# Batch 1 of an attention kernel: q and k cast into SBUF and transposed on TensorE instead of by DMA, additive masks built on GpSimd

## The chip, the cores and the metric

One core of a Trainium2 chip runs the whole kernel. The time is the device time of one execution in microseconds. Before the change the median of 13 runs is 360.24 us (356.14 to 362.5). PE is TensorE's matmul side, PEld its weight loads, DVE is VectorE, ACT ScalarE, POOL GpSimd, SP SyncE (here it only issues DMAs).

## The reference

Attention over q, k, v of shape (8 batches, 8 heads, 576 positions, 64), then a feed-forward layer:

```python
scores = q @ k.T / 8                      # per batch and head
rel = pos[:, None] - pos[None, :]
plain:   0 <= rel < 32                    # heads 0 to 3
dilated: 0 <= rel < 128 and rel % 4 == 0  # heads 4 to 7
attn = softmax(where(mask, scores, -1e9)) @ v
x = attn, heads side by side              # 4608 tokens x 512
h = x @ w_in                              # 512 x 2048
out = (h * sigmoid(beta * h)) @ w_out     # 2048 x 512
```

Inputs and output are fp32; the kernel multiplies in bf16.

## The kernel before

**Stages.** A batch has 576 tokens; the feed-forward part runs over 9 groups of 512 tokens. For each group there are 16 h slots (`slot_h`: four matmuls of 512 columns, a tanh on ACT, line 486, and a multiply on DVE, line 489, that leaves `g`) and 16 o slots (`slot_o`: four matmuls each, line 512, scaled out by ACT, stored by SP). The attention of batch t + 1 is issued between the slots of group t, and batch 0 before them all. Every engine has its own queue and takes its instructions in the order in which the program issues them, so the order of work is the order in the code: lists of step names (`FIRST` for batch 0, `SECOND` for batch 1, `THIRD` for batch 2, `STEPS` for the rest) say in which order a batch's steps come, and the loop at the end says after which slot how many of them are issued (at t = 0 the function `first`, later a share by `WORK`). At t = 0 the slots are 16 h and 12 o; the first 21 have no step behind them, the next has 28, and each one after that 5.

**Steps.** A step is a letter and digits. x is a pair of heads: 0 and 1 plain, 2 and 3 dilated.
- `K`, `Q` (batch 0 only): q or k, already in SBUF as bf16 with tokens on the partitions (`tok`, loaded and cast by POOL's DMA queue, line 258), is transposed on PE (lines 344, 353) and copied out of PSUM into `kd`, `qzd` (dilated) or `k1`, `q1` (plain). K has one copy, on DVE or ACT. Q has two, one on DVE and one on ACT, into two halves whose rest is zero.
- `S`: a score tile, with exp on ACT (line 411). In batches 0 and 1 an additive mask (`neg`) is first put into PSUM by a matmul with the identity (line 386); from batch 2 on POOL multiplies the exp by a 0/1 mask instead (line 413).
- `V`: scores times v, with a column of ones for the sum; DVE takes the reciprocal (line 434) and multiplies (line 438).
- `X`: transposed on PE (line 448) and copied by ACT into `xT`, the input of the feed-forward part.
- `d`, `k`, `q` (batch 1 on): the spreads, DVE copies (lines 285, 289, 297) of DMA-transposed q and k into the zero-padded `qzd`, `kz`, `qq`. For these batches POOL's queue casts q and k into a scratch in HBM (`cast_qk`, line 245) and SP's queue transposes them from there into SBUF (lines 267, 276).
- `v`: v cast from its fp32 staging (`vd_st`, `vp_st`).
- `m0`, `m1`, `M0`: masks finished on DVE. POOL builds 0/1 masks (lines 165 to 200) and DVE turns them into additive ones (`negate`, line 162). `M0` also zeroes `kz[0]`, whose storage `k1` of batch 0 used.

The plain heads of batch 0 keep their keys and queries in natural order; from batch 1 on they are split into even and odd positions, as the DMA transpose gives them, which is why `mask_p` has an even and an odd part and a score tile of plain heads takes four matmuls (line 398) instead of two (line 392).

**Queues.** POOL issues the loads that cast; a load waits until the eighth before it has landed. `gate` is a one-element POOL copy that waits for a DMA transpose to land, so that the DMAs behind it in POOL's program don't start sooner.

Of the kernel before, what the change touches and what calls it, by code (L numbers as in the profile page):

```python
# [23 lines left out]
    "K2 K3 Q2 Q3 m0 S20 S21 S22 S23 v0 v1 K0 K1 m1 V20 S30 V21 S31 V22 S32 V23 S33 Q0 Q1 V30 S00 V31 "  # L24
    "X20 S01 V32 S02 V33 v2 S10 X21 S11 V00 X30 S12 V01 X31 V10 X00 V11 X01 X10 X11"
).split()
SECOND = (
    "M0 d0 d1 S20 S21 S22 S23 S30 S31 S32 S33 v3 k0 k1 V20 V21 V22 V23 q0 q1 q2 q3 V30 S00 V31 S01 "
    "X20 v2 V32 S02 V33 S10 X21 S11 V00 X30 S12 V01 X31 V10 X00 V11 X01 X10 X11"
# [8 lines left out]
def kernel(  # L38
# [10 lines left out]
    nc = tc.nc  # L49
# [41 lines left out]
    def bank(dt=FP32):  # L91
# [27 lines left out]
    k1 = kz[0][:].rearrange("p a b c d -> p (a b c d)")[:, 0:2 * (WIN + S)].rearrange(  # L119
        "p (x t) -> p x t", x=2)  # L120
    q1 = qq[0][:].rearrange("p a b c d -> p (a b c d)").rearrange("p (x h t) -> p x h t", x=2, h=2)
    plain_T = {n: const([P, c0 + 2 * S], BF16, f"{n}pT") for n, c0 in (("k", WIN // 2), ("q", 0))}
    xT = const([P, NKT, B * S], BF16, "xT")

# [3 lines left out]
    for m, (n, x) in enumerate((n, x) for n in "kq" for x in range(2)):  # L128
# [3 lines left out]
    mask_1, neg_1_pp, neg_1_fp = (  # L132
        xT[:, m, 2 * S:2 * S + 4 * QT].rearrange("p (a n) -> p a n", a=2) for m in range(3))
    neg_1 = {"FP": neg_1_fp, "PP": neg_1_pp}
# [8 lines left out]
    def zeros(i):  # L143
        if i == 0:
            for x in range(4):
                nc.vector.memset(pt[x][:, pt_w[x]:], 0.0)
            for x in range(2, 4):
                nc.vector.memset(pt[x][64:96, 8 * DQ[0]:8 * DQ[0] + 32], 0.0)
            nc.vector.memset(k1[:, :, 0:WIN], 0.0)
            nc.vector.memset(q1[64:128, :, 0], 0.0)  # L150
            nc.vector.memset(q1[0:64, :, 1], 0.0)
        nc.vector.memset(qzd[i][64:128, 0], 0.0)
        nc.vector.memset(qzd[i][0:64, 1], 0.0)
        if i:
            zeros_kz(i)
            nc.vector.memset(plain_T["k"][:, 0:WIN // 2], 0.0)
        nc.vector.memset(vp[i][:, :, :, D:D + 1], 1.0)
        nc.vector.memset(vd[i][:, :, :, :, D:D + 1], 1.0)


    def negate(t, m):
        nc.vector.tensor_scalar(
            out=t, in0=m, scalar1=-1.0, scalar2=NEG, op0=ALU.add, op1=ALU.mult)

    def build_masks_d():

        for hf, lo in ((0, 0), (1, DQ[0] - DO[1])):
            flat = mask_d[hf][:].rearrange("p a b n -> p (a b) n")
            nc.gpsimd.memset(flat, 1.0)
            nc.gpsimd.affine_select(  # L170
                out=flat, in_=flat, pattern=[[0, 4], [1, DQ[hf]]], base=lo,
                channel_multiplier=-1, compare_op=ALU.is_ge, fill=0.0)
            nc.gpsimd.affine_select(
                out=flat, in_=flat, pattern=[[0, 4], [-1, DQ[hf]]], base=WIN - 1 - lo,
                channel_multiplier=1, compare_op=ALU.is_ge, fill=0.0)


    def build_mask_1():
        flat = mask_1.rearrange("p a (b n) -> p (a b) n", b=2)
        nc.gpsimd.memset(flat, 1.0)  # L180
        nc.gpsimd.affine_select(
            out=flat, in_=flat, pattern=[[0, 4], [-1, QT]],
            base=-1, channel_multiplier=1, compare_op=ALU.is_ge, fill=0.0)
        nc.gpsimd.affine_select(
            out=flat, in_=flat, pattern=[[0, 4], [1, QT]],
            base=WIN, channel_multiplier=-1, compare_op=ALU.is_ge, fill=0.0)
# [14 lines left out]

    def finish_masks_1(b, n, eng):
        if n == 0:
            for hf in range(2):
                negate(neg[f"d{hf}"][:], mask_d[hf][:].rearrange("p a b n -> p a (b n)"))
        else:
            for n in ("PP", "FP"):
                negate(neg_1[n], mask_1)
            nc.vector.memset(neg_1["FP"][0:WIN, 0], -NEG)

    def finish_masks(b, n, eng):
        zeros_kz(0)
        pp, fp = mask_p["PP"], mask_p["FP"]
        nc.vector.tensor_copy(
            out=pp[64:128].rearrange("p a b e u -> p (a b) e u"), in_=mask_t[64:128])
        nc.vector.tensor_copy(out=fp[:], in_=pp[:])
        for e in range(2):
            nc.vector.memset(fp[64 * e:64 * e + WIN // 2, 0], 0.0)
        for n in ("PP", "FP"):
            negate(neg[n][:], mask_p[n][:].rearrange("p a b e u -> p a (b e u)"))  # L220
# [31 lines left out]
    def load_tok(n, x):  # L252
        dst = tok[n, x]
        R, T = (72, 8) if x else (64, 9)
        src = {"q": q, "k": k}[n][0, 4 * x:4 * x + 4].rearrange("h (a T) d -> a h (T d)", T=T)
        for lo, hi in ((0, 64), (64, R)):
            if lo < hi:
                nc.gpsimd.dma_start(out=dst[lo:hi], in_=src[lo:hi])
# [44 lines left out]
    def load_vp_1(eng, n, m, p=0):  # L303
        eng.dma_start(
            out=vp_st[0][:].rearrange("p h i d -> p (h i) d")[p:P, n:n + m],
            in_=bass.AP(tensor=v.tensor, offset=v[0, 0].offset + (QT * n - WIN + p) * D,
                        ap=[[D, P - p], [QT * D, m], [1, D]]))

# [26 lines left out]
    kd[0] = kd_pool.tile([P, 2, 4, CT], BF16, name="kdT")  # L335
# [22 lines left out]
    def step_k(b, x):  # L358
        eng = nc.scalar if x % 2 else nc.vector
        if x < 2:  # L360
            copy_on(eng)(out=k1[:, x, WIN:].rearrange("p (a e) -> p a e", e=9),
                         in_=transposes_p("k", x))
        else:
            copy_on(eng)(out=kd[0][:, x - 2].rearrange("p h (a w) -> p h a w", w=2),
                         in_=transposes_d("k", x - 2))

    def step_q(b, x):
        tv = transposes_p("q", x) if x < 2 else transposes_d("q", x - 2)
        for hf in range(2):
            rows = slice(64 * hf, 64 * hf + 64)  # L370
            out = (q1[rows, x, hf].rearrange("p (a e) -> p a e", e=9) if x < 2 else
                   qzd[0][rows, hf, x - 2].rearrange("p h (a w) -> p h a w", w=2))
            copy_on(nc.scalar if hf else nc.vector)(out=out, in_=tv[rows])

    def step_s(b, x, j):
# [8 lines left out]
        if b < 2:  # L384
            rhs = neg_1[key] if b == 0 and x < 2 else neg[key]
            nc.tensor.matmul(sc[0:K, :, 0:2 * n], lhsT=ident_b[0:K, 0:K], rhs=rhs[0:K],  # L386
                             start=True, stop=False)
        for a in range(2):
            if x < 2:
                i = 2 * j + a  # L390
                if b == 0:
                    nc.tensor.matmul(
                        sc[:, a, 0:2 * n], lhsT=k1[:, x, i * QT:i * QT + P],
                        rhs=q1[:, x, :, i * QT:(i + 1) * QT], start=False, stop=a == 1)
                    continue
                for h2 in range(2):
# [5 lines left out]
                        start=b > 1, stop=b > 1 or a + h2 == 2)  # L402
# [39 lines left out]
    def step_x(b, x, j):  # L442
# [10 lines left out]
        if x < 2 and b == 0:  # L453
# [11 lines left out]
    BRING = {"d": spread_dil, "k": spread_k, "q": spread_q, "v": cast_v, "m": finish_masks_1, "M": finish_masks}  # L465

    def attention_step(b, name):
        if name[0] in STEP:
            STEP[name[0]](b, *[int(c) for c in name[1:]])
        else:  # L470
            eng = (nc.scalar if b == 0 and name == "q0" or b == 1 and name == "v2" else
# [64 lines left out]
    def extras(b):  # L536
# [4 lines left out]
        if b + 1 < B:  # L541
# [7 lines left out]
            if b == 1:  # L549
                at("V21", load_vd, b + 1, G)  # L550
            name = "V21" if b > 2 else "S32" if b > 1 else "V30"
            for kind in "kq":
                at(name, load_dil, b + 1, kind)
            for kind in "kq":
                at(name, load_plain, b + 1, kind)
# [18 lines left out]
    V.memset(vp_st[0][0:WIN, 0, 0], 0.0)  # L574
    for n in "kq":
        load_tok(n, 1)
    make_identity(nc, ident_b[:])
    make_identity(nc, ident_f[:])
    load_vd(0, SQ)
    load_vp_1(SQ, 0, 1, WIN)  # L580
    load_vp_1(A, 1, 2 * NI - 1)
    SQ.dma_start(out=beta_row[:], in_=moe_beta.rearrange("(f p) -> f p", p=P))
    zeros(0)
    zeros(1)
    load_tok("k", 0)
    build_masks_d()
    load_tok("q", 0)
    load_vp_1(G, 2 * NI, 2 * NI)
    build_mask_1()
    for g in range(4):  # L590
        load_w_in(g)
    for name in FIRST:
        if name == "S33":
            build_beta()
        if name == "v2":
            G.memset(vd_st[64:96, 1], 0.0)
            build_masks_p()
        attention_step(0, name)
    for g in range(2):
        load_w_out(g)  # L600
    load_vd(1, G)
    for n in range(4):
        load_vp(1, G, n * NI, NI)
    for kind in "kq":
        cast_qk(1, kind)
    for kind in "kq":
        load_dil(1, kind)
    for kind in "kq":
        load_plain(1, kind)
    gate(raw[1, "d"][0:1, 0, 0, 0:1])  # L610
# [4 lines left out]
    for kind in "kq":  # L615
        cast_qk(2, kind)


    at_once = [3, 2] + [1] * (NTT - 3) + [4]
    WORK = {"S": 3, "V": 3, "X": 2, "d": 3, "k": 0, "q": 0, "v": 0, "M": 0}  # L620
    left = []
    first = lambda n: 0 if n < 21 else 28 + 5 * (n - 21)
# [62 lines left out]
```

## Time and profile before

| | us |
|---|---|
| median of 13 runs | 360.24 (356.14 to 362.5) |
| the profiled execution | 361.1 |
| its span in the trace | 359.3 |
| first matmul starts | 10.01 |
| first matmul of the feed-forward part | 32.0 |
| first matmul of group 1 | 72.7 |
| PE / DVE / ACT / POOL busy | 321.0 / 210.6 / 191.9 / 134.5 |

The page cuts the span into 40 slices of 9 us, with the busy share of each engine in tenths; the row PEclk is the granted clock of PE. The chain of work that ended last follows each piece of work back to what released it. A group of instructions is given with its line, engine, operation and tile, the number of instructions and their time; "[3.05 <-DVE qq L297]" says that the engine sat idle for 3.05 us before it, until line 297 on DVE had written `qq`. Starts are microseconds from the start of the span. Times of matmuls overlap, so that the distance from one start to the next says more of their rate than the length of one.

### The profile page before, as it was taken

Reading aid. Unit: us, or ns where it says so; the run is one execution under the profiler, and the core shown is the slowest. Engines: PE = TensorE matmul, PEld = TensorE weight load, DVE = VectorE, ACT = ScalarE, POOL = GpSimd, SP = SyncE. Lnnn points to the kernel's source line nnn. Section 1 sums busy time; section 2 is a strip of 40 time slices with the busy share of each in tenths; the row PEclk is TensorE's granted clock in tenths of the full one; section 3 lists DMA queues with packets and bytes.
Section 4 is the critical chain, followed back from the end, with each engine's and each line's share of the span. In section 5 each row is a group of like instructions: output and inputs, shape, how many; then the busy total and the mean of one; then the engine's idle time right before and its main releaser. Section 6 shows DMA issues by size and latency. Waiting matters only on the chain.

```text
span 359.3 us, 6041 instructions
## 1 busy us (share of the span) xinstructions
PE 321.0 (89%) x2265; PEld 169.0 (47%) x2265; DVE 210.6 (59%) x439; ACT 191.9 (53%) x365; POOL 134.5 (37%) x170
## 2 busy tenths in 40 slices
PE   0798996988867998799999999999999999999995
PEld 0674444534442554355545554555455544444442
DVE  6554787459894579356955693679356444334400
ACT  1455734666531676266656665666566555435511
POOL 8993045016273535353464355346333200000000
PEclk9998997899996999899999999999999999999999
DMA  8999999998976890799269928991101111111031
GB/s 173 208 206 212 169 151 204 196 216 168 192 121 132 168 194 0 161 163 176 52 128 182 193 50 161 189 197 31 35 29 31 30 30 31 58 30 31 29 80 66
DMA packets 67757, 43.77 MB, mean 122 GB/s; under 512 B 52288, under 2 KB 61712, under 8 KB 67280
## 3 DMA queue, kind: packets, MB, share of 16 engines
q1 hardware_dynamic: 58864, 25.99, 37.0%
q0 software_dynamic: 7440, 17.04, 26.0%
q10 hardware_dynamic: 1424, 0.36, 0.6%
q8 instruction: 17, 0.28, 0.4%
q14 instruction: 12, 0.10, 0.1%
HBM read 39.32 MB, written 17.69 MB: 159 GB/s over the span
## 4 chain that ended last, share of the span: by engine, by line
PE 76%; DVE 15%; ACT 3%; DMA 2%; issue 1%; POOL 0%; DVEq 0%; ACTq 0%; POOLq 0%
PE h_ps L481 30%; PE o_ps L512 28%; DVE qq L297 4%; DVE xs L438 3%; PE at L431 3%; PE at L481 3%; PE h_ps L512 3%; PE at L448 3%; DVE g L489 3%; DMA xT<-in_k_dram 2%; PE at L405 2%; DVE kz L289 2%; PE at L398 2%; PE at L386 1%; ACT osb L517 1%
## 5 line engine op out<-in xcount | busy, mean ns | idle before, releaser
L489 DVE SCALAR_TENSOR_TENSOR g<-tnh,h_ps 128x512 bf16<-128x512 bf16 x132 | 90.2, 685 | 98.7 <-ACT tnh L486 98.2
L481 PE MATMUL h_ps<-xT,w_in_bf 128*128 128x512 bf16 x528 | 134.3, 383 | 3.5 <-DVE g L489 3.2
L512 PE MATMUL o_ps<-w_out_bf,g 128*128 128x512 bf16 x512 | 132.2, 387 | 3.3 <-ACT osb L517 3.2
L486 ACT ACTIVATE tnh<-h_ps,beta_half 128x512 bf16<-128x512 f32 x132 | 90.7, 687 | 61.9 <-PE h_ps L481 55.4
L512 PEld LDWEIGHTS <-g 128*128 128x128 bf16 x576 | 53.4, 99 | 58.5 <-issue 9.5
L481 PEld LDWEIGHTS <-w_in_bf 128*128 128x128 bf16 x576 | 53.3, 99 | 57.3 <-issue 7.8
L411 ACT ACTIVATE pt<-at 128x384 bf16<-128x384 f32 (+2 forms) x112 | 48.1, 440 | 29.1 <-PE at L398 13.5
L413 POOL TENSOR_TENSOR pt<-pt,mask_d 96x384 bf16<-96x384 bf16 (+1 forms) x48 | 35.7, 755 | 58.1 <-ACT pt L411 57.5
L438 DVE TENSOR_TENSOR xs<-at,rcp 96x256 bf16<-96x256 f32 (+2 forms) x96 | 44.5, 463 | 15.6 <-PE at L448 11.6
L413 POOL TENSOR_TENSOR pt<-pt,mask_PP 128x384 bf16<-128x384 bf16 x24 | 23.6, 982 | 36.4 <-ACT pt L411 36.3
L517 ACT ACTIVATE osb<-o_ps 128x512 f32<-128x512 f32 x32 | 19.1, 597 | 27.5 <-PE o_ps L512 27.5
L431 PEld LDWEIGHTS <-pt 128*128 128x128 bf16 (+2 forms) x448 | 25.8, 102 | 16.0 <-POOL pt L413 2.7
L448 PE MATMUL at<-ident_b,xs 96*128 96x96 bf16 (+1 forms) x224 | 20.0, 208 | 7.5 <-DVE xs L438 5.1
L297 DVE COPY qq<-qpT 64x1152 bf16<-64x1152 bf16 x28 | 24.8, 884 | 0.6
L448 PEld LDWEIGHTS <-xs 96*128 96x128 bf16 (+1 forms) x224 | 13.5, 100 | 18.4 <-DVE xs L438 10.5
L405 PEld LDWEIGHTS <-kdT 128*96 128x96 bf16 (+1 forms) x128 | 15.6, 130 | 12.0 <-issue 2.5
L431 PE MATMUL at<-vd,pt 96*128 96x65 bf16 (+1 forms) x256 | 19.9, 202 | 0.7 <-POOL pt L413 0.6
L458 ACT COPY xT<-at 128x288 bf16<-128x288 bf16 x28 | 10.8, 398 | 16.9 <-PE at L448 16.8
L405 PE MATMUL at<-qzd,kdT 128*96 128x192 bf16 (+1 forms) x128 | 19.1, 239 | 0.7 <-DVE qzd L285 0.7
L413 POOL TENSOR_TENSOR pt<-pt,mask_FP 128x384 bf16<-128x384 bf16 x12 | 12.8, 1063 | 15.6 <-ACT pt L411 15.6
L434 DVE RECIPROCAL rcp<-at 96x4 f32<-96x4 f32 (+2 forms) x96 | 16.6, 173 | 3.0 <-PE at L431 2.4
L398 PE MATMUL at<-qq,kz 128*128 128x96 bf16 x168 | 14.7, 213 | 3.0 <-DVE qq L297 3.0
(94 smaller groups left out, 221.6 us busy)
## 6 DMA issues: line engine op xcount, KB each, us to landing
qk<-in_k_dram POOLq DMA_DIRECT2D x7, 576.0 KB, 5.6
qk<-in_q_dram POOLq DMA_DIRECT2D x7, 576.0 KB, 8.0
vp_st<-in_v_dram SPq DMA_DIRECT2D x10, 384.0 KB, 8.6
vd_st<-in_v_dram SPq DMA_DIRECT2D x6, 384.0 KB, 5.1
w_in_bf<-in_moe_w_in_dram POOLq DMA_DIRECT2D x4, 512.0 KB, 9.5
w_out_bf<-in_moe_w_out_dram POOLq DMA_DIRECT2D x4, 512.0 KB, 7.8
out_dram<-osb SPq DMA_DIRECT2D x8, 256.0 KB, 3.0
vd_st<-in_v_dram SPq DMA_DIRECT2D x6, 320.0 KB, 6.3
```

The source lines that it names most:

```text
L297: copy_on(eng)(out=qq[b % 2][64 * hf:64 * hf + 64, :, :, e], in_=raw[b, "q"][64 * e:64 * e + 64].rearrange("p (h i u) -> p h i u", h=4, i=NI))
L405: nc.tensor.matmul(sc[0:K, a, 0:2 * n], lhsT=kd[b][:, rp, h4, DO[hf]:DO[hf] + K], rhs=qzd[b % 2][:, :, rp, h4, hf * DQ[0]:hf * DQ[0] + n], ...
L411: nc.scalar.activation(out=w, in_=sc[0:K, :, 0:2 * n], func=ACT.Exp, scale=SCALE)
L413: nc.gpsimd.tensor_tensor(out=w, in0=w, in1=mask[0:K], op=ALU.mult)
L431: nc.tensor.matmul(pv[:, a, h2, :], lhsT=pt[x][0:K, c:c + P], rhs=rhs, start=True, stop=True)
L438: nc.vector.tensor_tensor(out=xs_t[b, x, jx][:, a0:a0 + m], in0=pv[0:n, :, :, 0:D], in1=rcp[0:n, 0:m].unsqueeze(3).to_broadcast([n, m, 2, ...
L448: nc.tensor.transpose(xp[:, a * n:(a + 1) * n], xs[:, a].rearrange("p h d -> p (h d)"), ident_b[0:n, 0:n])
L481: nc.tensor.matmul(hps, lhsT=w_in_bf[:, kt, fb * P:(fb + 1) * P], rhs=xT[:, kt, t * NTOK:(t + 1) * NTOK], start=(kt == 0), stop=(kt == NKT ...
L486: nc.scalar.activation(out=tnh[:], in_=hps, func=ACT.Tanh, scale=beta_half[:, fb:fb + 1])
L489: nc.vector.scalar_tensor_tensor(out=g[:], in0=tnh[:], scalar=1.0, in1=hps, op0=ALU.add, op1=ALU.mult)
L512: nc.tensor.matmul(ops[:], lhsT=g_t[t, fb][:, tb * P:(tb + 1) * P], rhs=w_out_bf[:, fb, :], start=(fb == 0), stop=(fb == NFB - 1))
L517: nc.scalar.mul(out=osb[:], in_=ops[:], mul=0.5)
```

## The change

Batch 1 takes the path of batch 0. Its q and k are cast by POOL's queue straight into the `tok` tiles (which batch 0 has done with), and `SECOND` has K and Q steps in place of d, k, q and M. `k1` and `q1` become lists, one for each of the two buffers, so the plain heads of batch 1 too have natural order, two matmuls to a score tile and the copy of `xT` without the even and odd split. The additive masks are built whole by POOL, ahead of the first steps; the 0/1 masks, needed from batch 2 on, are built by POOL much later, and finished there instead of on DVE. `zeros(1)` moves on DVE's queue from the start to behind batch 0's attention; `kz[0]` is zeroed at step X11 of batch 1 and `kz[1]` at step S30 of batch 2. The load of v for batch 0's plain heads is one load on POOL's queue after the token tiles, where ACT's queue had one half and POOL's the other; plain v of batch 1 is one load instead of eight. In the POOL queue order the eight loads of `vp_st` for batch 2 and its two casts to HBM keep their place at the end; `v0`, `v1` come first in `FIRST`. At t = 0 the steps of batch 1 are issued four after each slot, from slot 15 on.

```diff
-    "K2 K3 Q2 Q3 m0 S20 S21 S22 S23 v0 v1 K0 K1 m1 V20 S30 V21 S31 V22 S32 V23 S33 Q0 Q1 V30 S00 V31 "
-    "X20 S01 V32 S02 V33 v2 S10 X21 S11 V00 X30 S12 V01 X31 V10 X00 V11 X01 X10 X11"
+    "v0 v1 K2 K3 Q2 Q3 S20 S21 S22 S23 S30 S31 K0 K1 S32 V20 S33 V21 Q0 Q1 V22 V23 S00 V30 "
+    "S01 V31 X20 S02 v2 V32 S10 V33 X21 S11 V00 X30 S12 V01 X31 V10 X00 V11 X01 X10 X11"
 ).split()
 SECOND = (
-    "M0 d0 d1 S20 S21 S22 S23 S30 S31 S32 S33 v3 k0 k1 V20 V21 V22 V23 q0 q1 q2 q3 V30 S00 V31 S01 "
-    "X20 v2 V32 S02 V33 S10 X21 S11 V00 X30 S12 V01 X31 V10 X00 V11 X01 X10 X11"
+    "K2 K3 Q2 Q3 v0 v1 S20 S21 S22 S23 K0 K1 S30 V20 S31 V21 S32 V22 S33 V23 Q0 Q1 V30 S00 "
+    "V31 X20 v2 S01 V32 S02 V33 S10 X21 S11 V00 X30 S12 V01 X31 V10 X00 V11 X01 X10 X11"
...
+    def band(t, w, lo, hi, yes, no):
+        flat = t.rearrange("p a (b n) -> p (a b) n", n=w)
+        nc.gpsimd.memset(flat, yes)
+        nc.gpsimd.affine_select(
+            out=flat, in_=flat, pattern=[[0, 4], [1, w]], base=-lo,
+            channel_multiplier=-1, compare_op=ALU.is_ge, fill=no)
+        nc.gpsimd.affine_select(
+            out=flat, in_=flat, pattern=[[0, 4], [-1, w]], base=hi,
+            channel_multiplier=1, compare_op=ALU.is_ge, fill=no)
...
+    def build_neg_d():
+        for hf, lo in enumerate(LO):
+            band(neg[f"d{hf}"][:], DQ[hf], -lo, WIN - 1 - lo, 0.0, -NEG)
...
+    def build_neg_p():
+        band(neg["PP"][:], QT, -WIN, -1, 0.0, -NEG)
+        nc.gpsimd.tensor_copy(out=neg["FP"][:], in_=neg["PP"][:])
+        nc.gpsimd.memset(neg["FP"][0:WIN, 0], -NEG)
...
-                if b == 0:
+                if b < 2:
                     nc.tensor.matmul(
-                        sc[:, a, 0:2 * n], lhsT=k1[:, x, i * QT:i * QT + P],
-                        rhs=q1[:, x, :, i * QT:(i + 1) * QT], start=False, stop=a == 1)
+                        sc[:, a, 0:2 * n], lhsT=k1[b][:, x, i * QT:i * QT + P],
+                        rhs=q1[b][:, x, :, i * QT:(i + 1) * QT], start=False, stop=a == 1)
...
             if b == 1:
-                at("V21", load_vd, b + 1, G)
+                at("X20", load_vd, b + 1, G)
+                at("X11", zeros_kz, 0)
+            if b == 2:
+                at("S30", zeros_kz, 1)
...
+    load_vd(0, SQ)
+    load_vp_1(0, SQ, 0, 1, WIN)
+    SQ.dma_start(out=beta_row[:], in_=moe_beta.rearrange("(f p) -> f p", p=P))
     for n in "kq":
-        load_tok(n, 1)
+        load_tok(0, n, 1)
     make_identity(nc, ident_b[:])
...
-    zeros(0)
-    zeros(1)
-    load_tok("k", 0)
-    build_masks_d()
-    load_tok("q", 0)
-    load_vp_1(G, 2 * NI, 2 * NI)
-    build_mask_1()
+    for n in "kq":
+        load_tok(0, n, 0)
+    build_neg_d()
+    load_vp_1(0, G, 1, 4 * NI - 1)
+    build_neg_p()
     for g in range(4):
         load_w_in(g)
+    make_identity(nc, ident_f[:])
+    zeros(0)
     for name in FIRST:
         if name == "S33":
             build_beta()
...
     for g in range(2):
         load_w_out(g)
+    for x in (1, 0):
+        for n in "kq":
+            load_tok(1, n, x)
+    G.memset(vd_st[64:96, 1], 0.0)
     load_vd(1, G)
-    for n in range(4):
-        load_vp(1, G, n * NI, NI)
-    for kind in "kq":
-        cast_qk(1, kind)
-    for kind in "kq":
-        load_dil(1, kind)
-    for kind in "kq":
-        load_plain(1, kind)
-    gate(raw[1, "d"][0:1, 0, 0, 0:1])
+    load_vp_1(1, G)
+    zeros(1)
+    V.memset(plain_T["k"][:, 0:WIN // 2], 0.0)
     for g in range(2, 4):
         load_w_out(g)
     for n in range(4):
         load_vp(2, G, n * NI, NI)
     for kind in "kq":
         cast_qk(2, kind)
+    build_masks_d()
+    build_masks_p()
...
-    first = lambda n: 0 if n < 21 else 28 + 5 * (n - 21)
+    first = lambda n: 0 if n < 15 else 4 * (n - 14)
```

## The prediction

> **What bounds the kernel now.** I read the top of the page first, then the work of each engine in cut-out stretches, then the chain that ended last, then the engines' own rows in order of time.
>
> ```profile
> span 359.3 us, 6041 instructions
> PE 321.0 (89%) x2265; PEld 169.0 (47%) x2265; DVE 210.6 (59%) x439; ACT 191.9 (53%) x365; POOL 134.5 (37%) x170
> PE   0798996988867998799999999999999999999995
> PEclk9998997899996999899999999999999999999999
> ```
>
> From slice 13 on (about 115 us) PE is at 9 in every slice: the steady state, bound by matmuls, 34.3 us per group of 512 tokens. The change touches nothing there. Whatever it does, it does in the first 115 us, which I cut at PE's own boundaries: A, until the first transpose at 10.0; B, attention of batch 0 (10.0 to 32.7); C, sixteen h slots of group 0 (to 47.56); D, twelve o slots of group 0 with attention of batch 1 among them (47.56 to 72.83); E, group 1 with attention of batch 2 (72.83 to 115.4). The stretches (columns: length, then busy time and count of PE, PEld, DVE, ACT, POOL, then clock, DMA share, GB/s):
>
> ```profile
> 47.56:72.83 25.27, 21.22 (x187) 12.70 (x186) 16.32 (x43) 11.15 (x26) 10.28 (x15) 0.86 1.06 193
> 72.83:115.40 42.57, 33.28 (x238) 16.98 (x236) 33.10 (x58) 20.75 (x41) 19.31 (x21) 0.94 0.87 162
> ```
>
> In D, PE has much less to do than its 21.22 us say. At full rate 4 matmuls of 512 columns take 0.86 us (chain), so 12 o slots are 10.4. Attention by its warm cadences: dilated scores with their masks 2.0 (53.36 to 55.37), plain ones 6 x 0.33, V 8 x 0.12 and 4 x 0.18, X about 1.2: 6.9. That is 17.3 of 25.3; 8.0 us are lost. The chain says to what (start, length, what):
>
> ```profile
> 48.30 0.69 DVE g L489
> ...
> 49.20 0.70 DVE kz L140
> ...
> 53.29 1.42 DVE vd L330
> ...
> 59.59 0.47 DVE qq L297
> 60.05 0.04 issue
> 60.09 0.48 PE at L398 x4
> ```
>
> For 11.8 us (48.30 to 60.05) DVE alone carries the end: zeroing kz, finishing masks, spreading the DMA-transposed q and k. PE then runs dry, and afterwards runs at half rate. The PE rows show both (start, busy, then shape; in brackets the wait):
>
> ```profile
> 13.79 0.53 PE L405 MATMUL at<-qzd,kdT 128*96 128x192 bf16 x2
> 53.52 0.33 PE L405 MATMUL at<-qzd,kdT 128*96 128x192 bf16 x2
> 60.09 0.48 PE L398 MATMUL at<-qq,kz 128*128 128x96 bf16 x4 [3.05 <-DVE qq L297]
> 61.55 1.91 PE L512 MATMUL h_ps<-w_out_bf,g 128*128 128x512 bf16 x4
> ```
>
> The same pair takes 0.53 in B and 0.33 in D (0.32 against 0.165 start to start). B is at half rate from 10 to 27.9 although the clock row gives it 9; and the o slot at 61.55 takes 1.71 on the chain for 0.86. So D's 8.0 is 3.05 of wait, about 3.2 of half rate (60.1 to 66.5), and 1.7 of small waits.
>
> **The change, part by part.** *A: the first loads.* The load of 352 KB on ACT's queue goes; its data joins a POOL load behind the four token tiles. Rows 5 to 10 us moved 212 GB/s, so 352 KB in front of k's landing (the chain's 7.72 us of DMA) are worth up to 1.7. Bounds 0 and 1.7; I take 1.4, since it did start ahead of k (0.98 against 1.33) and landed at 8.2, before k at 9.9. v0 and v1 now stand ahead of K2 in DVE's queue and wait for vd_st: its halves landed 4.0 and 6.7 us after their issues, at 4.8 and 8.0 or so, and earlier without the 352 KB; two casts of 0.68 are over before K2 has anything to copy (k's landing plus 0.7). Hidden, with about 1 us to spare; later by more than that it would delay K2 one for one. The POOL issues moved up (q's plain tile past the masks, 0.6) are behind k's in the queue.
>
> *B: masks.* The additive masks come from POOL in the 2.5 us that the multiplicative ones took (5.40 to 8.05), so DVE's four negations and a memset (0.36, 0.42, 0.22 in groups) vanish. PE's wait of 1.19 on neg_d is replaced by a wait for ACT's half of qzd, which ended at 13.3 with scores starting at 13.99: 0.6 gained. Six scores now run before K0, and V22, V23 between Q1 and S00, where PE waited 0.41 and 0.26: 0.3 more. Matmul counts don't change. I take 0.9 (0.5 to 1.5). POOL's v2 cast waits for the bigger vp load: the bytes ahead of it are the same 2.6 MB, so about 16 us as now, needed by V00 at 25.
>
> *C.* zeros(1), some 3.1 us by its rows 4.71 to 8, moves behind batch 0's last DVE work, where DVE waited 3.16 for the first tanh. Nothing; without that cover the first g would be late by up to 3 us, of which the two-deep banks and 0.17 of slack per g would return 2.7 by C's end.
>
> *D.* Out: M0 (two memsets, three copies and so on), the spreads d, k, q of 0.94, 1.35 and 1.85, on DVE; four DMA transposes on SP (41.4 to 50), whose data landed up to 53, and POOL's gate of 12.0 us. In: six token loads (1152 KB) behind w_out. By 205 GB/s after vp (16 us) come w_in 2048, w_out 1024, these 1152: landed near 36.5, vd_st at 40, vp_st at 44. They are needed at 46 and after, so also the waits for eight loads outstanding on POOL's queue are covered. In on PE: 104 transposes. 32 of 72 columns: between 0.035 (half of B's 0.070) and 0.070; 72 of 64 columns: between 0.030 (the warm V matmuls: six in 0.18) and 0.042 (B). 3.3 to 5.3 us, I take 3.7, warm. In on DVE: two copies of 0.70 and four of 0.70, 4.3; on ACT two of 0.64 and four of 0.65, 3.9. PE needs 17.3 + 3.7 = 21.0. What it still waits for: S20 needs K2, Q2, Q3 through DVE, then ACT's half after DVE's half (as at 12.66). From the last h slot, t0: tanh and g 1.4, K2 2.1, Q2 2.8, ACT's half 3.5. PE has transposes 1.3, one o slot 0.86 and a mask 0.16 for it, until 2.35: waits 1.15, and 0.4 for S21. Later an o slot stands between every four steps, and DVE (14.2 us with V's divisions) and ACT (13.6) keep up; some 0.9 for the tail of X. D is 23.5 instead of 25.3: 1.8 gained.
>
> [...] The row: 17.9 us of nearly unbroken small matmuls at half rate (10 to 27.9), and again 6.5 us after the gap at 57. [...]
>
> *E.* Zeroing kz: one pair (2 x 0.70) at D's end, where DVE waited 3.71: nothing. The other pair stands at S30 of batch 2, in a stretch where DVE is the bound (33.1 of 42.6 busy, 9.6 of 10 from 80 to 90). It delays every g and V behind it, and PE waits for g. DVE has 1.2 us idle from 94 to 97 to give back. 0.2 to 1.4, or 3.1 if it tips a half-rate window; I take 1.0. Batch 2's casts end near 58 instead of 69, and its transposes follow earlier, but nothing in E waited for them (DVE's qzd at 80.24 had no wait ahead): 0. The multiplicative masks, 5 to 6 us of POOL after those casts, are over by 60; first used at 82. SP's queue holds nothing else then.
>
> **Sum.** -1.4 - 0.9 - 1.8 + 1.0 = -3.1. The profiled execution took 361.1 (span 359.3, 1.8 around it): 358.0. It lies 0.9 above the median of 360.24, so the forecast for a median is 357.1. The runs of before spread from 356.1 to 362.5, in two clumps; 0.5% (1.8 us) is about what can be told from no change.
>
> **Rivals.** *D at half rate (slower).* Its place is D's first 14 us, small matmuls between o slots. [...] For it: B's row. Against: after o slots came back at 65.4 the rate was full. *The gain stays on paper (same).* k lands at 9.9 anyway because its own small pieces, not the 352 KB, set it, and D stays at 25.3 as the copies' hand-over DVE to ACT eats the shorter DVE chain: -0.9 + 1.0 = about 0, 360.3; with A real, 358.9. For it: k took 8.3 us for 256 KB, more than its bytes need. [...]
>
> **How the numbers follow.** The main case 0.46, paper 0.22, half rate 0.19, more 0.13. Faster by over 0.5%: nearly all of the main case and of the last, 0.59; same 0.22; slower 0.19. The main case alone spans 355.3 to 358.9. The range takes in the fast rival's time and the paper rival, and stops between it and the half-rate rival: 353.5 to 362.0.
>
> **What would show it.** First transpose at 8.6 rather than 10.0 (A). First h slot near 30.4 (B). From the last h slot to the first h of group 1, 23.5 us, 512-column matmuls at 0.216 each, no PE wait over 1.5 and none on a spread (D). E 43.6, with DVE still the releaser. The prediction is wrong if token tiles of batch 1 land after 46, if o slots in D take 1.7, or if E grows by more than 2.

## The result, and the profile after

The median fell from 360.14 us (48 runs, 356.14 to 362.5) to 353.43 us (11 runs, 350.65 to 356.19). The ratio is 0.9815, with a 95% interval of 0.9774 to 0.9855: faster by 1.9%, some 6.7 us, where 3.1 was forecast. The sign is right, but less than half of the gain was forecast: 353.43 lies just under the range's low end of 353.5.

The top of the page of the kernel after (busy time of each engine, then PE's busy tenths and the granted clock in 40 slices):

```profile
span 351.7 us, 6237 instructions
PE 316.8 (90%) x2357; PEld 168.6 (48%) x2357; DVE 208.9 (59%) x430; ACT 195.8 (56%) x371; POOL 135.9 (39%) x178
PE   0998989986768997999999999999999999999995
PEclk9999999999998999999999999999999999999999
```

PE executes 92 more matmuls and yet is busy 4.2 us less: its matmuls have become shorter, not fewer. The clock row says why. Before, five of its digits were under 9 (slices 3, 6, 7, 12 and 16, counted from 0); now one is.

I cut both profiled executions at the same places of PE's program:

| stage | before | after | change | forecast |
|---|---|---|---|---|
| A, to the first transpose | 10.01 | 8.47 | -1.54 | -1.4 |
| B, attention of batch 0, to the first h | 21.99 | 20.01 | -1.98 | -0.9 |
| C, sixteen h slots | 15.38 | 14.25 | -1.13 | 0 |
| D, twelve o slots with batch 1 | 25.29 | 24.03 | -1.26 | -1.8 |
| E, group 1 with batch 2 | 42.70 | 43.52 | +0.82 | +1.0 |
| group 2 | 35.79 | 33.39 | -2.40 | 0 |
| groups 3 to 8 | 208.14 | 208.03 | -0.11 | 0 |
| span | 359.3 | 351.7 | -7.6 | -3.1 |

Two of the three surprises, C and group 2, are in stretches where PE runs the same matmuls in the same order in both kernels. In group 2 the rows differ in nothing but the rate. Here are the last two o slots of groups 1 and 2, eight equal matmuls each, of the kernel before (PE's rows in order of time: start, busy, shape, count):

```profile
111.96 3.62 PE L512 MATMUL o_ps<-w_out_bf,g 128*128 128x512 bf16 x8
147.86 3.44 PE L512 MATMUL o_ps<-w_out_bf,g 128*128 128x512 bf16 x8
```

and of the kernel after, with the rows of D that answer the forecast's:

```profile
8.47 2.33 PE L328 MATMUL at<-ident_b,xT 72*128 72x72 bf16 x32 [8.47 <-POOL neg_d L160]
...
42.73 1.21 PE L328 MATMUL at<-ident_b,xT 72*128 72x72 bf16 x32
...
46.38 0.33 PE L388 MATMUL at<-qzd,kdT 128*96 128x192 bf16 x2 [1.42 <-ACT qzd L357]
...
55.82 0.33 PE L375 MATMUL at<-qq,kz 128*128 128x192 bf16 x2 [0.74 <-ACT qq L357]
55.99 1.02 PE L495 MATMUL o_ps<-w_out_bf,g 128*128 128x512 bf16 x4
...
107.19 3.25 PE L495 MATMUL o_ps<-w_out_bf,g 128*128 128x512 bf16 x8
...
141.94 1.89 PE L495 MATMUL o_ps<-w_out_bf,g 128*128 128x512 bf16 x8
```

Eight matmuls took 3.44 us at 147.86 before and 1.89 at 141.94 after, behind the same wait of 1.35. In D the longest wait is now 1.42 instead of 3.05, and the o slot behind it takes 1.02 instead of 1.91. The transposes ran at full rate, 32 in 1.04 us from start to start, where the same 32 took 2.14 in B.

The chain of the kernel after in the same place (start, length, what):

```profile
43.65 0.36 DVE g L472
...
44.25 0.75 DVE kdT L348
45.00 1.33 DVE qzd L357 x2
46.33 0.02 issue
46.36 0.64 ACT qzd L357
...
54.36 0.76 DVE qq L357
```

DVE alone carries the end for 2.7 us (43.65 to 46.33), where it was 11.8.

The stretches of half rate can be cut out (columns: stretch, length, then busy time and count of PE, PEld, DVE, ACT, POOL, then granted clock, DMA share, GB/s). The kernel before, from the time at which it first has the full rate (28.1):

```profile
31.50:35.00 3.50, 3.16 (x10) 1.23 (x11) 0.34 (x2) 1.34 (x3) 1.34 (x3) 0.51 1.04 191
35.00:58.80 23.80, 21.31 (x127) 10.80 (x126) 19.82 (x39) 12.79 (x23) 8.89 (x13) 1.00 1.01 168
58.80:65.70 6.90, 5.61 (x44) 3.57 (x44) 2.62 (x9) 3.69 (x7) 3.09 (x5) 0.51 1.13 219
...
110.00:116.90 6.90, 5.58 (x18) 2.25 (x19) 1.48 (x5) 1.39 (x3) 0.84 (x2) 0.51 0.88 172
...
147.60:151.00 3.40, 3.36 (x11) 1.43 (x12) 0.00 (x0) 0.41 (x2) 0.00 (x0) 0.50 0.96 201
```

and the kernel after, which has one such stretch:

```profile
106.60:110.10 3.50, 3.12 (x11) 1.28 (x12) 0.32 (x1) 0.75 (x2) 0.00 (x0) 0.52 0.83 174
```

They are 3.4 us or twice that; counted as windows of 3.4 us, they are six before and one after. The scatter of one kernel goes with them as well: the six runs of the third experiment below go from 351.59 us at a mean granted clock of 0.997 to 358.71 at 0.986. The two profiled runs here stood at 0.971 before and 0.995 after. They are no odd pair: the 57 runs of the kernel before that were taken beside the experiments lie between 0.971 and 0.990, and of twelve runs of the kernel after nine stand at 0.995 and three at 0.986. But six windows is the most that a run of before shows; at 0.990 it has about two (1% of some 354 us, twice that at half rate).

PE was busy for 3.16 + 5.61 + 5.58 + 3.36 = 17.7 us in the windows before and 3.12 in the one after. Half of that is what the half rate can have cost: 8.9 and 1.6. The difference of 7.3 is nearly the whole 7.6 us. That leaves the rest of the change, loads, masks, transposes, waits and zeros, with a balance near zero, since A and B already give 3.5 and must then be spent again in D and E. This is the theory that I took to the chip.

### The profile page after: what moved, and what is told of

Read it like the earlier page. It is cut to its first block, busy times and chain, and to the rows that moved or that the text cites. A ratio compares the mean times of both kernels' runs of the same rounds, so it can differ in the third digit from the quotient of the medians.

```text
span 351.7 us, 6237 instructions
## 1 busy us (share of the span) xinstructions
PE 316.8 (90%) x2357; PEld 168.6 (48%) x2357; DVE 208.9 (59%) x430; ACT 195.8 (56%) x371; POOL 135.9 (39%) x178
## 4 chain that ended last, share of the span: by engine, by line
PE 78%; DVE 12%; ACT 3%; DMA 2%; POOL 2%; issue 1%; SPq 0%; POOLq 0%; DVEq 0%; ACTq 0%
PE h_ps L464 30%; PE o_ps L495 29%; PE h_ps L495 4%; PE at L414 3%; DVE qq L279 3%; PE at L464 3%; PE at L431 3%; DVE xs L421 2%; PE at L388 2%; DVE g L472 2%; DMA vd_st<-in_v_dram 2%; DVE kz L271 2%; PE at L369 1%; PE at L337 1%; PE at L381 1%
## 5 line engine op out<-in xcount | busy, mean ns | idle before, releaser
L464 PE MATMUL h_ps<-xT,w_in_bf 128*128 128x512 bf16 x528 | 132.8, 379 | 5.0 <-DVE g L472 4.5
L495 PE MATMUL o_ps<-w_out_bf,g 128*128 128x512 bf16 x512 | 130.3, 382 | 3.3 <-ACT osb L500 3.2
L495 PEld LDWEIGHTS <-g 128*128 128x128 bf16 x576 | 52.5, 98 | 54.6 <-issue 6.2
L279 DVE COPY qq<-qpT 64x1152 bf16<-64x1152 bf16 x24 | 21.9, 911 | 0.5
L441 ACT COPY xT<-at 128x288 bf16<-128x288 bf16 x24 | 9.4, 397 | 16.6 <-PE at L431 16.6
L495 PE MATMUL h_ps<-w_out_bf,g 128*128 128x512 bf16 x64 | 15.5, 379 | 0.0
```

The source lines that it names most:

```text
L279: copy_on(eng)(out=qq[b % 2][64 * hf:64 * hf + 64, :, :, e], in_=raw[b, "q"][64 * e:64 * e + 64].rearrange("p (h i u) -> p h i u", h=4, i=NI))
L464: nc.tensor.matmul(hps, lhsT=w_in_bf[:, kt, fb * P:(fb + 1) * P], rhs=xT[:, kt, t * NTOK:(t + 1) * NTOK], start=(kt == 0), stop=(kt == NKT ...
L495: nc.tensor.matmul(ops[:], lhsT=g_t[t, fb][:, tb * P:(tb + 1) * P], rhs=w_out_bf[:, fb, :], start=(fb == 0), stop=(fb == NFB - 1))
```

## The experiments

*Theory W (work):* the gain is work and waits taken off the path, stage by stage, as the forecast had it. *Theory C (clock):* most of it is windows of half rate (3.4 us each, as above) that the gaps of PE in the kernel before bring on and the changed order avoids. No experiment leaves computation out; the fillers are extra matmuls whose result nobody reads:

```python
def fill(n):
    fp = bank()
    for _ in range(n):
        nc.tensor.matmul(fp, lhsT=w_in_bf[:, 0, 0:P], rhs=w_in_bf[:, 0, 0:NTOK],
                         start=True, stop=True)
```

Ratios are against the kernel before on the same chip. The runs of one kernel scatter by 2 to 8 us, and there are six to twelve of each, so an effect under 2 us is read from the profile rather than from medians.

**1. Only the loads and the additive masks.** The kernel before, with the loads and POOL-built additive masks of batch 0 and the new order of `FIRST` (`zeros(1)` stands ahead of K0); batch 1 keeps its DMA transposes.

```diff
-    load_vp_1(A, 1, 2 * NI - 1)
-    build_masks_d()
+    build_neg_d()
-    load_vp_1(G, 2 * NI, 2 * NI)
-    build_mask_1()
+    load_vp_1(G, 1, 4 * NI - 1)
+    build_neg_1()
...
+            build_masks_d()
             build_masks_p()
```

> The kernel before with only the first part of the change: ACT's load of v joins the POOL load behind the token tiles, the additive masks of batch 0 are built by POOL, FIRST has the new order. Batch 1 keeps its DMA transposes and spreads. Theory W (the gain is the work taken off the path, stage by stage): first transpose near 8.5 and first h slot near 28.5 to 29.5, so 3.0 to 3.5 us of the 6.7 are here, 357 for a median. Theory C (most of it is half-rate windows of PE that batch 1's gap causes): D still has its gap of 3 us and its two windows, and so the gain is at most the 1.5 us of the loads, 358.5 or more.

Measured: 361.29 us, ratio 1.005 (1.0005 to 1.0095): slower by half a percent. The first transpose came at 8.43 and the first h at 28.96, so A and B kept their gain, but D grew to 29.1 us. Its PE rows:

```profile
53.25 0.48 PE L424 MATMUL at<-qzd,kdT 128*96 128x192 bf16 x2 [2.20 <-DVE qzd L304]
...
61.13 0.48 PE L417 MATMUL at<-qq,kz 128*128 128x96 bf16 x4 [3.07 <-DVE qq L316]
```

The gap of the kernel before is still there (3.07), and a second one stands ahead of it. The chain (start, length, what) shows where that came from:

```profile
39.69 0.54 POOL qk L264
40.22 7.86 DMA qk<-in_q_dram
...
48.10 4.15 DMA qdT<-qk
```

The cast of q was issued at 40.22, where the kernel before issued it at 37.16. On POOL the multiplicative dilated masks, built later now, stood ahead of the loads of `w_out` (issued at 24.42 instead of 21.65), and the last four loads ahead of the casts waited 0.54, 4.34, 1.51 and 0.73 us for earlier loads to land (1.65, 2.17, 1.22 and 0.81 in the kernel before). So these parts by themselves made the kernel slower, by a cause that this edit brought in and the change doesn't have; run 2 takes the loads alone.

**2. Only the 352 KB load.** The kernel before with the one load moved and nothing on POOL reordered.

```diff
-    load_vp_1(A, 1, 2 * NI - 1)
...
-    load_vp_1(G, 2 * NI, 2 * NI)
+    load_vp_1(G, 1, 4 * NI - 1)
```

> The kernel before with the loads alone: 352 KB of v go from ACT's queue at the start to POOL's behind the token tiles; masks, order and POOL's casts for batch 1 stay. Theory W: first transpose at 8.5, all of the 1.5 us kept: 358.5. Theory C together with the reading of the loads-and-masks run (batch 1's data there came no sooner, so PE waited 2.20 us more for it): the 1.5 us end in the wait for batch 1's spreads, 359.5 to 360.5.

Measured: 356.87 us against 358.3 for the kernel before on the same chip, ratio 0.9926 (0.9886 to 0.9966). The first transpose came at 8.19, and the gap of D stayed:

```profile
58.84 0.48 PE L398 MATMUL at<-qq,kz 128*128 128x96 bf16 x4 [3.15 <-DVE qq L297]
```

Theory W was right here and C wrong: the loads' gain reaches the end even with the gap in place. The loss of run 1 is then most likely that of the reordered POOL queue, as its rows say.

**3. Filling the gap, and nothing else.** The kernel before with thirteen fillers where PE ran dry.

```diff
             if b == 1:
+                at("q0", fill, 13)
                 at("V21", load_vd, b + 1, G)
```

> The kernel before, with 13 matmuls of 512 columns that nobody reads put on PE between V23 and S00 of batch 1, where it waits 3.05 us for the spreads of q. Theory W: PE waits for DVE anyway and nothing is gained, 360; if the filler overruns the gap, up to 1 us is lost. Theory C: the gap itself is not shortened, but the half-rate windows behind it (58.8 to 65.7) go: D 2 to 3 us shorter, 357.5 to 358.

Measured: 354.57 us, ratio 0.9833 (0.9766 to 0.9901). Thirteen useless matmuls give 5.6 us, more than C expected, and W expected nothing.

```profile
55.00 2.97 PE L539 MATMUL at<-w_in_bf 128*128 128x512 bf16 x12
...
58.73 0.33 PE L398 MATMUL at<-qq,kz 128*128 128x96 bf16 x4 [0.48 <-DVE qq L297]
```

The fillers (one record of the thirteen is missing) take the place of the wait (3.05 became 0.48), the pair behind them takes 0.33 instead of 0.48, and D takes 22.8 us instead of 25.3. The old path, at full rate, is shorter in D than the new one (24.0). The windows at 31 and 147 were gone in this profile too; that can't all be the fillers' doing, since the one at 31 comes before them. In this profile 2.5 of the gain are D's; how much of the rest the fillers brought is not shown.

**4. The control: three fillers.** The same edit with three.

```diff
+                at("q0", fill, 3)
```

> A control for the filler: the kernel before with 3 unread matmuls in the first gap instead of 13, 0.65 us of work in 3.05. Theory C: too little to count as busy, the half-rate windows come as before: 359 to 360. If it is something else about the filler (another bank taken, another order of waits) that made the time shorter, it is here too: 355.

Measured: 359.98 us, ratio 1.0002 (0.9961 to 1.0043), with the same windows as before.

```profile
59.99 0.48 PE L398 MATMUL at<-qq,kz 128*128 128x96 bf16 x4 [2.42 <-DVE qq L297]
...
61.45 1.91 PE L512 MATMUL h_ps<-w_out_bf,g 128*128 128x512 bf16 x4
```

With a wait of 2.42 the rate still goes, with one of 0.48 it doesn't. That the fillers shift code or banks is an unlikely cause, since these do it too.

**5. Both gaps filled against the change with its tail filled.** To compare the two kernels with no window on either side once B has its full rate: the kernel before with thirteen fillers in D and ten ahead of X01 of batch 2, and the kernel after with those ten.

```diff
             if b == 1:
+                at("q0", fill, 13)
...
+            if b == 2:
+                at("X01", fill, 10)
```

> The kernel before, with the 13 unread matmuls between V23 and S00 of batch 1 and 10 more ahead of X01 of batch 2: nothing of the change, only PE kept busy in its two longest gaps. Theory C: 352.5 to 354, at or near the kernel after (353.4), with two half-rate windows fewer than with the first filler alone (354.6). If the change has a worth of its own beside the rate, this stays 2 us or more above the kernel after with its tail filled (351.8).

> The kernel after, with 10 unread matmuls of 512 columns ahead of X01 of batch 2, where PE waits 2.30 us for DVE. Theory C: the one half-rate window left (106.6 to 110.1) goes, and with it 1.5 us in E and the chance of one in the next group: 351 to 352, less scatter. Theory W: nothing, 353.4.

Measured: 354.16 us, ratio 0.9881 (0.9828 to 0.9934), for the kernel before with fillers, and 351.76, ratio 0.981 (0.9756 to 0.9863), for the one after. Stages B, D and E of the first (columns as above):

```profile
10.02:31.84 21.82, 18.27 (x231) 14.86 (x232) 13.89 (x38) 12.12 (x27) 16.24 (x25) 1.00 1.21 215
...
46.09:68.97 22.88, 21.06 (x198) 12.54 (x200) 16.58 (x43) 10.93 (x27) 10.28 (x15) 1.00 1.02 193
68.97:110.16 41.19, 33.49 (x244) 17.52 (x247) 33.35 (x58) 20.75 (x41) 19.27 (x21) 1.00 1.00 174
```

and of the second:

```profile
8.57:28.33 19.76, 18.01 (x232) 14.67 (x232) 11.31 (x32) 12.15 (x27) 14.07 (x23) 1.00 1.17 201
...
42.57:66.61 24.04, 21.10 (x275) 13.92 (x279) 14.69 (x36) 15.09 (x33) 11.85 (x24) 1.00 1.06 185
66.61:108.70 42.09, 33.65 (x244) 17.51 (x246) 34.35 (x61) 20.86 (x42) 19.19 (x21) 1.00 0.87 155
```

Without windows the change gives 1.45 in A and 2.06 in B, and costs 1.16 in D and 0.90 in E; C (14.25 and 14.24) and group 2 (33.38 and 33.41) are equal. The balance is 1.45 us, and the spans, 351.8 and 350.1, say 1.7; the medians say 2.4, from six runs each that scatter by 4 us. So the 2 us or more that were to show a worth of its own are met by the medians and not by the profiles. Beside the windows the change is worth 1.5 to 2.4 us, not 7, and part of that is rate too: in B full rate came 17.7 us after the first transpose in the first and 15.3 in the second. The rest was the windows. (The clock of 1.00 shown for B is not real in its first part: the rows there run at half rate, as before.)

**6. The change with the steps in a lump.** The kernel after with the issue order of the kernel before: nothing after the first 21 slots, then 28 steps at once.

```diff
-    first = lambda n: 0 if n < 15 else 4 * (n - 14)
+    first = lambda n: 0 if n < 21 else 28 + 5 * (n - 21)
```

> The kernel after, with batch 1's steps issued as before: none before slot 21, then 28 at once, then 5 per slot. The transposes on TensorE stay. Theory W: it is the DVE chain of the spreads that went, the order of issue is worth little: within 1 us of the kernel after (353.4). Theory C: without o slots between the small matmuls PE falls to half rate in D and waits for copies in one block: D 2 to 4 us longer, 355.5 to 357.5.

Measured: 357.63 us, ratio 0.9941 (0.9896 to 0.9986), 4.2 above the kernel after. The profiled run has D at 25.8 instead of 24.0, with 1.15 more of waits on PE (0.64, 1.22, 0.18, 1.12, 0.39 and 0.27 add to 3.82, against 1.42, 0.17, 0.74 and 0.34), and no window in D, though it has two later (87.5 and 108.0). Spreading the steps over the slots is thus worth more than half of what the whole change brings, by the medians. W's "within 1 us" is wrong, and C's half rate in D did not come: the 1.8 by which D is longer lie in waits and small stretches. That the 4.2 of the medians are rate is not shown, as the one run with a profile accounts for 1.7.

**7. The load put back.** The kernel after with the 352 KB on ACT's queue again.

```diff
+    load_vp_1(0, A, 1, 2 * NI - 1)
...
-    load_vp_1(0, G, 1, 4 * NI - 1)
+    load_vp_1(0, G, 2 * NI, 2 * NI)
```

> The kernel after, with 352 KB of v back on ACT's queue at the start. Both theories: first transpose near 10.0 instead of 8.5, 1.5 us longer, 355; if it is the small pieces of k and not the bytes ahead of them, no difference. If the phase of the clock windows rules, the time does not follow the first transpose.

Measured: 358.11 us, ratio 0.9873 (0.978 to 0.9965), in six runs from 352.84 to 360.73: this doesn't settle a price. The profile does for A (first transpose 9.75, so 1.3 for the load), and it holds a surprise. In B:

```profile
15.23 0.52 PE L369 MATMUL at<-neg_d,ident_b 96*96 96x384 bf16 x1
15.55 0.52 PE L388 MATMUL at<-qzd,kdT 128*96 128x192 bf16 x2
16.00 1.27 PE L337 MATMUL at<-ident_b,xT 64*64 64x64 bf16 x36
...
18.22 1.01 PE L337 MATMUL at<-ident_b,xT 64*64 64x64 bf16 x36
```

The second set of 36 transposes takes 1.01 instead of 1.57: full rate from 16.7, only 7 us after the first transpose, where the kernel after needs 16. B took 17.6 us, the span 351.3, less than the 351.7 of the kernel after. When B gets its rate is a matter of some us and no plain function of the order of the work.

**8. PE warmed while the loads run.** The kernel after with twenty 512-column matmuls on a constant, from 1.54 us on.

```diff
+    V.memset(w_out_bf[:, 0, :], 1.0)
+    wps = psum_o.tile([P, HD], FP32, name="o_ps")
+    for _ in range(20):
+        nc.tensor.matmul(wps[:], lhsT=w_out_bf[:, 0, 0:P], rhs=w_out_bf[:, 0, :], start=True, stop=True)
     V.memset(warm[:], 0.0)
```

> The kernel after, with 20 matmuls of 512 columns that nobody reads put on PE while it waits for the first loads (0 to 8.5 us). Theory C: batch 0's attention (8.5 to 28.5, at half rate until 24.6 in the profile) starts at full rate: stage B 20 us becomes 15 to 17, the time 349 to 351, and the runs scatter less, as the point at which PE gets its full rate no longer depends on the phase of the windows. Theory W: B is a chain of copies and small matmuls, hardly shorter: 353. If the filler does not warm PE by 8 us it delays the first transpose by up to 1.5 us.

Measured: 352.56 us, ratio 0.9818 (0.9772 to 0.9865); C had expected 349 to 351.

```profile
13.26 1.02 PE L337 MATMUL at<-ident_b,xT 64*64 64x64 bf16 x36
...
16.30 0.23 PE L206 MATMUL at<-ident_f,beta_row 16*128 16x16 f32 x1 [1.60 <-POOL ident_f masks.py:199]
...
16.88 1.37 PE L337 MATMUL at<-ident_b,xT 64*64 64x64 bf16 x36
...
18.61 0.51 PE L369 MATMUL at<-neg_FP,ident_b 128*128 128x384 bf16 x1
```

The warm-up works: the first set of 36 takes 1.02. Then PE waits 1.60 us for `ident_f`, which the change had moved behind the loads of `w_in` on POOL, and from 17.2 to 24.0 it is at half rate again. The first h starts at 27.43, one us earlier and no more. In the kernel after this wait doesn't show, as PE gets there later.

**9. The masks negated on DVE again.** The kernel after with 0/1 masks from POOL and DVE's negations.

```diff
-            band(neg[f"d{hf}"][:], DQ[hf], -lo, WIN - 1 - lo, 0.0, -NEG)
+            band(mask_d[hf][:].rearrange("p a b n -> p a (b n)"), DQ[hf], -lo, WIN - 1 - lo, 1.0, 0.0)
...
-    "v0 v1 K2 K3 Q2 Q3 S20 S21 S22 S23 S30 S31 K0 K1 S32 ...
+    "v0 v1 K2 K3 Q2 Q3 m0 S20 S21 S22 S23 m1 S30 S31 K0 K1 S32 ...
```

> The kernel after, with the masks of batches 0 and 1 built as 0/1 by POOL and negated by DVE as before (behind Q3 and behind S23). Theory W: the 1.19 us wait comes back, first h slot 0.6 to 0.9 later, 354 to 354.5. Theory C: the same 0.6, or more if PE gets its full rate a window later: up to 356.

Measured: 354.62 us, ratio 0.9881 (0.9818 to 0.9944), 1.2 above the kernel after with overlapping intervals. The wait of 1.19 for `neg_d` is back, the first h comes at 28.80 instead of 28.48. So the masks themselves are worth 0.3 in that profile, not their wait.

**10. kz[1] zeroed by POOL.** Taken out of the stretch where DVE is the bound.

```diff
-            if b == 2:
-                at("S30", zeros_kz, 1)
+                at("X11", zeros_kz, 1, G)
```

> The kernel after, with kz[1] zeroed by POOL at X11 of batch 1 instead of by DVE at S30 of batch 2. Both theories: DVE's 1.4 us leave the stretch in which it is the bound, E 0.8 to 1.4 us shorter, 352 to 352.6; by theory C the PE wait of 1.70 for g goes too, which should not matter for the rate, since no window turns on it.

Measured: 351.98 us, ratio 0.9804 (0.9754 to 0.9854), 1.45 under the kernel after. In the kernel after PE waits for a g that the zeroing delays:

```profile
86.27 1.02 PE L464 MATMUL h_ps<-xT,w_in_bf 128*128 128x512 bf16 x4 [1.70 <-DVE g L472]
```

and in this one the same slot starts with no such wait:

```profile
84.48 1.02 PE L464 MATMUL h_ps<-xT,w_in_bf 128*128 128x512 bf16 x4
```

E takes 41.7 us instead of 43.5, although two windows of half rate fall into its end in this profile and only one in that of the kernel after.

**11. All that helped, together.** The kernel after with the warm-up, `ident_f` built ahead of `neg_d`, kz[1] zeroed by POOL, and ten fillers ahead of X01 of batch 2.

```diff
+    make_identity(nc, ident_f[:])
     build_neg_d()
...
-    make_identity(nc, ident_f[:])
...
+                at("X11", zeros_kz, 1, G)
             if b == 2:
-                at("S30", zeros_kz, 1)
+                at("X01", fill, 10)
```

> The kernel after with three things together: 20 unread matmuls ahead of the first transpose, with the small identity built before the masks (PE waited 1.60 us for it when warm), kz[1] zeroed by POOL, and 10 unread matmuls ahead of X01 of batch 2. Theory C: B stays at full rate from 8.5 on and takes 16 to 17 us instead of 18.9 to 20, E loses 0.8 to 1.4 and its half-rate windows: 346 to 348.5. Theory W: the sum of e6 alone, 352.

Measured: 349.31 us (346.62 to 350.83), ratio 0.973 (0.9677 to 0.9784): 2.7% under the kernel before, and 0.8 us above what was expected of theory C. Against the kernel after the medians are 1.2% apart, and the two intervals overlap by only 0.001. Its span and stage B:

```profile
8.61:24.59 15.98, 12.36 (x233) 9.87 (x232) 11.13 (x32) 11.54 (x27) 12.35 (x19) 1.00 1.15 198
```

B takes 16.0 us at full rate, with the same 231 matmuls or so that take 20.0 after and 22.0 before. PE is busy 12.4 instead of 18.3. The profiled run's span is 344.9 us; it was the fastest of the six.

## Why the prediction was right in sign and wrong in size

**Right, with their sizes.** A: 1.54 for 1.4, and the load alone accounts for it (1.8 in run 2, 1.3 in run 7). The token tiles of batch 1 landed by 39 us where 36.5 was said, and were needed at 42.7, so nothing waited for them. E: +0.82 for +1.0, by the step given: two zeroings of 0.70 delay a g, and PE waits for it. In D the transposes took 2.9 us for the 104 (1.04 for 32, two times 0.95 for 36) where 3.7 was taken and 3.3 was the low end, and no half-rate window fell there. That D would run at full rate throughout was an estimate that no run had shown. It did: its granted clock was 1.00 from 42.73 to 66.76. That this comes from the o slots between the small matmuls is not shown, since run 6 kept the rate in D with the small matmuls in a lump. B and run 4 show the other side: in B PE ran small matmuls almost without a break for 16 us at half rate, and in run 4 the rate went with a wait of 2.42 us. The 3.1 among E's bounds holds some 1.7 for a stretch at half rate, a price that no run shows as such: the one stretch of the kernel after is 3.5 us long with PE busy for 3.12, so at half rate it can have cost 1.6.

**Wrong: "The change touches nothing there."** The step that failed is the first one, which took everything from 115 us on for a steady state with PE at 9 in every slice, and with it put C and group 2 at nothing. The row itself was misread: it has an 8 at slice 15 and a 7 at slice 16, counted from 0, where group 2 ends. And PE's busy tenths can't tell 8 matmuls in 1.89 us from 8 in 3.44; the row of PEclk, in the same fence, had a 6 at slice 12 and an 8 at slice 16. In truth the steady state of the profiled execution began at 151 us, and it lost up to 8.9 us in four stretches of half rate, of which the forecast priced one, the 3.2 in D. The other three, behind the waits at 31, 111 and 147, stood in the trace. The profiled pair differs from the forecast by 4.5 us, -7.6 for -3.1; group 2's 2.4 and C's 1.1 are 3.5 of it, B's 1.1 the rest, and D and E nearly cancel what is left.

**D, nearly right for the wrong reason.** It was forecast at 23.5 and took 24.0. At the warm cadences used there its work is 10.4 + 6.9 + 2.9 = 20.2, its waits 1.59 for the dilated halves (1.55 forecast), 0.74 for the plain ones (left out) and 0.34 in the tail; 1.2 is in small stretches. But D did not get shorter by the path taken off DVE: the old path with fillers takes 22.8 to 22.9. All of D's gain is rate, about 2.5 us, less 1.2 for longer work and waits.

**B was undersized.** The forecast's 0.9 was for waits alone. Full rate comes 3.5 us sooner (24.6 for 28.1), of which 1.5 is A's; 2.0 us of PE at full instead of half rate is about 1 us more. Why it comes sooner is open: run 7 had it after 7 us, run 5's pair after 17.7 and 15.3.

**The rivals.** "D at half rate" did not happen. "The gain stays on paper" is wrong of the sum, and half right of D: what the shorter chain saved is eaten, but by the transposes. At full rate the old path has 17.3 us of work in 22.8, so 5.5 of waits and small stretches; the new one has 20.2 in 24.0, so 3.8. The 2.9 of transposes outweigh the 1.7 saved. An outcome faster than the main case was given 0.13. It came, at 353.43, and most of what the forecast missed is rate: the four stretches of half rate behind 28.1 us in the trace of before, 20.7 us in all, would have spoken for it.

**Which waits bring on a window.** The traces answer most of this. In the kernel before the stretches of half rate start at 31.5, 58.8, 110.0 and 147.6 us, so 27.3, 51.2 and 37.6 apart: 8, 15 and 11 times 3.41. In all fourteen profiles (the two kernels and the twelve runs above) the changes of rate fit such a grid of 3.41 us: run 8 has them at 7.0, 17.2, 24.0, 106.0 and 109.4, run 7 at 16.7, 105.4 and 108.8. Counted from the span's start, its points lie 0.8 us behind a whole multiple of 3.41 in the kernel before, 0.7 in the kernel after, 0.2 in run 8 and 3.0 in run 7. The losses of the rate can be set against how long PE was busy between two points of the grid. At the end of group 2 the same wait fell into one interval before:

```profile
146.88 0.30 PE L448 MATMUL at<-ident_b,xs 96*128 96x96 bf16 x3 [1.35 <-DVE xs L438]
...
144.18:147.59 3.41, 1.66 (x17) 0.76 (x15) 3.13 (x7) 0.77 (x2) 2.56 (x3) 1.00 0.61 132
```

and was split between two after:

```profile
141.04 0.30 PE L431 MATMUL at<-ident_b,xs 96*128 96x96 bf16 x3 [1.35 <-DVE xs L421]
...
137.25:140.66 3.41, 2.20 (x17) 0.99 (x16) 3.24 (x5) 0.88 (x3) 3.41 (x4) 1.00 0.25 77
140.66:144.07 3.41, 2.57 (x16) 1.28 (x17) 0.98 (x3) 1.00 (x3) 0.24 (x1) 1.00 0.94 173
```

PE was busy 0.49 of the interval before, and 0.65 and 0.75 of the two after. Between 32 and 340 us the fourteen profiles hold 21 losses of the full rate: 20 came behind an interval in which PE was busy 0.19 to 0.49 of the time, one behind 0.58 (run 4), and no interval under 0.50 kept the rate. So an interval need not be idle to cost the rate. D's gap left PE busy 0.44 of its interval (1.51 of 3.41 us), and filling it kept the rate. The 2.4 us of group 2 in the profiled pair go with where its wait fell on the grid; so may C's 1.1, as runs 3 and 5, the kernel before up to there, had no window at 31.

**What is open.** Among the small matmuls ahead of 32 us that share doesn't decide: the rate was lost behind 0.53 to 0.72 and kept behind 0.62 and more. Why B's first full rate comes when it does stays open too. So does a part of the 6.7 us: 1.5 to 2.4 are work and 2.5 are D's rate, but no run shows whether the other windows, some 2 us by the medians, are rarer because of the change or were rarer by chance in its runs.

## What to carry to other kernels

Before a stretch is called steady, compare the time of equal matmuls in it, not PE's busy share: a PE wait of 2 to 3 us can cost itself and then some 2.8 us of slower matmuls behind it (half of the 5.6 that PE was busy in the 6.9 us after D's gap). Take more than one profile, since the same wait can cost the rate in one and not in another (behind 1.35 us at the end of group 2, eight matmuls took 3.44 us before and 1.89 after). When a change shortens a kernel, fill the old gap with matmuls that nobody reads; if that alone brings most of the gain, the change was a cure for the rate, and cheaper cures may exist. Spread small matmuls between large ones (4.2 us by the medians of run 6, of which 1.7 are accounted for), and give PE something to do while the first loads run (in run 11, with `ident_f` built earlier as well, batch 0's attention took 16.0 us instead of 20.0).

## What was not expected of the hardware

- Small matmuls alone warm PE slowly and at no fixed time: full rate came 14.3 to 18.8 us after the first transpose in most profiled runs, and 7.0 in one. Twenty matmuls of 512 columns, begun at 1.54 us, had brought it by 7.0.
- Among small matmuls a wait of 1.60 us was enough to lose the rate for 6.8 us (run 8), while after the change's 1.42 in D, with o slots on both sides, it was kept. PE was busy 0.53 of the interval in the one and 0.57 in the other.
- The clock shown is 1.00 in the first part of B, although the pairs there take 0.53 us and later 0.33: the cadence of the rows is the better witness there.
